# The first weight fetches and the first chunk's k on ScalarE's DMA queue, six raw weight tiles instead of three

## The chip, the cores and the metric

The kernel runs on one core of a Trainium2 chip, as one launch. The metric is the device time of an execution in microseconds; the time before is the median of three runs, and one more execution was taken with the hardware profiler. The core has five engines that run in parallel and each work through their own instructions in order: TensorE (PE, with the weight load PEld shown apart), VectorE (DVE), ScalarE (ACT), GpSimd (POOL) and SyncE (SP). They wait for one another through semaphores. Transfers between HBM and SBUF are done by 16 DMA engines; an instruction on the queue of an engine, up to now always SP, issues them.

## The reference

Three stages follow each other, all in float32 (the weights come as float64):

```python
# 1: retention, 8 batches, 8 heads, 576 positions, head dimension 64
scores = np.matmul(q, k.transpose(0, 1, 3, 2)) / np.sqrt(64)
ret = scores * Dmat            # gamma[h] ** (i - j) for i >= j, else 0
x = np.matmul(ret, v)          # -> (4608, 512)
# 2: maxout layer, w1, w2, w3 (512, 768), w_out (768, 512)
h = np.maximum(np.maximum(x @ w1, x @ w2), x @ w3)
x = h @ w_out
# 3: bilinear layer, w1, w2 (512, 1024), w3 (1024, 1024), w_out (1024, 512)
out = ((x @ w1) * (x @ w2) @ w3) @ w_out
```

## The kernel before

**Work.** The 4608 tokens are taken in nine blocks of 512. The retention is computed in chunks of 128 or 64 positions with a carried state. The chunks are counted from 0 here: 0 to 3 have 128 positions each and fill the first block; chunk 4, the rest of the first batch, has 64. For each block the maxout layer then runs over six feature blocks f of 128 features and three weights i. Every product is done in three passes of split numbers: x is split into a high part xh and a rest xl, a weight into w1h and w1l (`products`, L332 to L341).

**A chunk.** `attend` records for each chunk: the fetch of q and k, four pieces each (`fetch_qk`, L233), of v and of kn, which is k with positions on the partitions (`fetch_kv`, L243); the scaling of q on POOL (L249); the transposes of q and k on VectorE into qt and kt (L256); the scores on PE (L262); the decay on VectorE (L266); the state product st on PE (L281) and, on VectorE, its addition to the carried state (L287) and the scaling of the state (L289); two copies of the state into `wide` on ScalarE (L293); the output o on PE (L271, L275); and the split of o into xh on ScalarE (L75 from L296) and xl on VectorE (L78 from L300).

**A weight unit.** The weights are float64 and are turned to float32 by `convert` (L120). A unit is 512 columns of 128 rows: `fetch` loads the raw 64-bit words into a tile named raw, in two DMAs of half the partitions; `words` makes two float tiles e and l from them on ScalarE (L134, L135); `scale` and `join` work on VectorE and, for some units, on POOL (L140 to L148); `done` splits the result w into w1h on ScalarE (L75) and w1l on VectorE or POOL (L78). There are 18 units of the first layer, unit 3f + i for feature block f and weight i. The tag raw has three buffers, so a fetch waits until the unit three places ahead of it in fetch order has been joined.

**What sets the order.** Each step is put on a list with a time number by `when` (L113); the list is sorted by it, and the steps are emitted in that order, so every engine's queue has a fixed order. The numbers of the startup stand in tables (`CHUNK_AT`, `W1_AT`, `W1_FETCH`, `HALF_AT`); the fetch of a unit has its own time, often far ahead of its work. All transfers go through `load` (L80) on SP.

**Completion counters.** Each DMA raises one of eight counters (DMAHW0 to DMAHW7) when it has landed. They are handed out in turn to the DMAs as they are emitted, whichever queue issues them, and a DMA waits on its queue until the preceding DMA with the same counter has landed. So a DMA can wait for another one with which it shares nothing else, and everything behind it on its queue waits too.

Of the kernel before, what the change touches and what calls it, by code (L numbers as in the profile page):

```python
# [11 lines left out]
I32 = mybir.dt.int32  # L12
# [10 lines left out]
P = 128  # L23
# [6 lines left out]
HALF_AT = [-6.14, -4.03, -0.84, -1.51, -0.17, 1.3, -0.43, 1.91, 3.01, -0.35, 2.74, 6.39]  # L30
L_DVE = [0, 0, 0, 0, 1, 0, 1, 1, 1, 0, 0, 0, 1, 0, 1, 1, 1, 1]
LO_DVE = [0, 0, 0, 0, 0, 0, 1, 0, 0, 0, 0, 0, 1, 1, 0, 0, 1, 1]
BACC = dict(dynamic_dma_scratch_size=512)


# [34 lines left out]
def tile_retention_maxout_bilinear(ctx: ExitStack, tc, a, out):  # L70
    nc = tc.nc
# [5 lines left out]
    def low(eng, dst, full, hi):  # L77
        eng.tensor_tensor(dst, full, hi.bitcast(F32), ALU.subtract)  # L78

    def load(dst, src):  # L80
        nc.sync.dma_start(out=dst, in_=src)  # L81

    first_ps = ctx.enter_context(ExitStack())
    ps_mm = first_ps.enter_context(tc.tile_pool(name="ps_mm", bufs=4, space=PSUM))
# [32 lines left out]
    T_BLK = 3 * KF1  # L117


    def convert(t, loads, done, eng=nc.gpsimd, lead=3):  # L120

        z = {}

        def fetch():
            z["raw"] = cv.tile([P, 1024], I32, tag="raw", name="raw", bufs=3)
            for dst, src in loads(z["raw"]):
                load(dst, src)

        def words():
            raw = z["raw"].rearrange("p (n t) -> p n t", t=2)  # L130
            z["hi"] = raw[:, :, 1]
            z["e"] = cv.tile([P, 512], F32, tag="e", name="e")
            z["l"] = cv.tile([P, 512], F32, tag="l", name="l")
            nc.scalar.activation(z["e"], raw[:, :, 1].bitcast(F32), AF.Copy, scale=2.0 ** -112)  # L134
            nc.scalar.activation(z["l"], raw[:, :, 0].bitcast(U32), AF.Copy, scale=2.0 ** -52)  # L135

        def scale():
            z["m"] = cv.tile([P, 512], I32, tag="m", name="m")
            e = z["e"].bitcast(I32)
            nc.vector.tensor_scalar(z["m"], e, 3, None, ALU.logical_shift_left)  # L140
            nc.vector.tensor_scalar(e, e, 3, 0x7F800000, ALU.logical_shift_left, ALU.bitwise_and)  # L141
            eng.tensor_tensor(z["l"], z["l"], z["e"], ALU.mult)  # L142

        def join():
            m = z["m"].bitcast(F32)
            nc.vector.tensor_tensor(m, m, z["l"], ALU.add)  # L146
            w = cv.tile([P, 512], I32, tag="w", name="w")
            nc.vector.scalar_tensor_tensor(w, z["hi"], -0x80000000, z["m"], ALU.bitwise_and, ALU.bitwise_or)  # L148
            z["w"] = w.bitcast(F32)

        when(t - lead, fetch)
        when(t - 1, words)
        when(t, scale)
        when(t + 1, join)
        when(t + 2, lambda: done(t + 2, z["w"]))
# [10 lines left out]
    def w1_unit(t, f, i, eng, eng2, lead):  # L166
        src = words_of(f"moe_w{i + 1}")[:, 2 * f * P:2 * (f + 1) * P].rearrange("(g c p) e -> g p c e", g=2, p=D)

        def loads(raw):
            r = raw.rearrange("p (c e) -> p c e", c=4)  # L170
            return [(r[D * g:D * g + D], src[g]) for g in range(2)]

        def done(t, w):
            copy_r(flat(w1h[f][:, i]), w)
            low(eng, flat(w1l[f][:, i]), w, flat(w1h[f][:, i]))

        convert(t, loads, done, eng2, lead)

    def rows_unit(t, src, dst):
        convert(t, lambda raw: [(raw, src)], lambda t, w: load(dst, w))  # L180
# [45 lines left out]
    def attend(n, t, t_st):  # L226
# [4 lines left out]
        z = {}  # L231

        def fetch_qk():  # L233
            z["q"] = at.tile([P, 4, G, 32], F32, tag="q", name="q", bufs=3)
            z["k"] = at.tile([P, 4, G, 32], F32, tag="k", name="k", bufs=3)
            for x in "qk":
                for g in range(2):
                    for e in range(2):
                        o = D * g + 32 * e
                        load(z[x][o:o + 32, :r], a[x][b, G * g:G * g + G, t0:t0 + c, 32 * e:32 * e + 32].rearrange(  # L240
                            "h (t T) d -> t T h d", T=r))

        def fetch_kv():  # L243
            for x in ("v",) if last else ("v", "kn"):
# [670 lines left out]
```

## Time and profile before

| | us |
|---|---|
| median of three runs (1381.56 to 1383.19) | 1382.69 |
| the profiled execution | 1383.29 |
| its span, first to last instruction | 1381.5 |
| PE busy | 1324.6 (96%) |
| VectorE busy | 821.9 (59%) |
| ScalarE busy | 469.5 (34%) |
| POOL busy | 498.4 (36%) |

The shares are means over very different stretches: the page's row of PE over 40 equal slices of 34.5 us begins with 3, 6, 8, 8 tenths and has 9 in nearly all others, while the row of VectorE begins with 3, then 9, 9, 9. A row of a view in order of time has the start in us from the beginning of the span, the duration, the engine, the line, the operation, the tile written and the tiles read, the shapes, how many instructions are merged in it, and in brackets the idle time of the engine ahead of it with what ended it. SPq rows are the issues of DMAs on SP's queue; they say nothing of when the data has landed.

### The profile page before, as it was taken

The page shows a single profiled execution, that of the slowest core. Times are in us where ns is not written, and L with a number is a line of the kernel's source. Part 1 is how long each engine was busy: PE and PEld are TensorE (multiplying, and loading weights), DVE is VectorE, ACT ScalarE, POOL GpSimd, SP SyncE. Part 2 cuts the span into 40 slices and gives each one's busy share as a digit, 9 for nine tenths or more (in the row PEclk, how much of TensorE's full clock was granted, in tenths as well). Part 3 has the DMA queues.
Part 4 walks back from the last instruction along what each step waited for, and adds up shares of the span by engine and source line. Part 5 has one row for each costly group of instructions (what it writes and reads, how often), then busy time and mean ns, then how long its engine had stood idle before and what let it go on. Part 6 is the DMA issues. An engine that isn't in the chain of part 4 may idle for free.

```text
span 1381.5 us, 23689 instructions
## 1 busy us (share of the span) xinstructions
PE 1324.6 (96%) x8904; PEld 1207.1 (87%) x8904; DVE 821.9 (59%) x1205; ACT 469.5 (34%) x933; POOL 498.4 (36%) x419
## 2 busy tenths in 40 slices
PE   3688999999999999999999999999999999899998
PEld 3676887888887888889999989999999999899998
DVE  3999677676676777423662343343343336688885
ACT  1433222322322222112543343332333324355553
POOL 2552233233223232113753343343343334444442
PEclk9799999999999999999999999999999999999999
DMA  8878678767777779234656542222223222445452
GB/s 149 156 156 167 161 172 185 179 162 181 170 179 165 151 152 197 66 107 147 207 177 218 175 159 94 81 75 81 75 75 104 75 91 74 127 148 167 153 168 93
DMA packets 368580, 194.09 MB, mean 140 GB/s; under 512 B 263888, under 2 KB 342352, under 8 KB 368464
## 3 DMA queue, kind: packets, MB, share of 16 engines
q1 hardware_dynamic: 368464, 192.57, 52.8%
q8 instruction: 70, 1.15, 0.4%
q14 instruction: 46, 0.38, 0.1%
HBM read 126.44 MB, written 66.06 MB: 139 GB/s over the span
## 4 chain that ended last, share of the span: by engine, by line
PE 86%; DVE 3%; DMA 2%; issue 1%; ACT 1%; SPq 0%; POOL 0%; DVEq 0%; ACTq 0%
PE ps_h L340 30%; PE ps_x L499 21%; PE ps_y L499 11%; PE ps_z L499 9%; PE ps_v L499 5%; PE ps_w L499 3%; PE sc L262 2%; PE o L271 2%; PE o L275 2%; PE st L281 1%; DMA raw<-in_moe_w_dram 1%; DMA z_d<-zo 0%; DMA gr<-g_d 0%; DMA hr<-h_d 0%; SPq L81 0%
## 5 line engine op out<-in xcount | busy, mean ns | idle before, releaser
L340 PE MATMUL ps_h<-xh,w1h 128*128 128x512 f32 (+1 forms) x672 | 264.5, 396 | 5.2 <-ACT xh L75 3.3
L340 PE MATMUL ps_h<-xh,w1l 128*128 128x512 f32 (+1 forms) x672 | 257.7, 385 | 3.1 <-POOL w1l L78 1.8
L142 POOL TENSOR_TENSOR l<-l,e 128x512 f32<-128x512 f32 x55 | 70.8, 1288 | 332.6 <-DVE e L141 276.3
L340 PE MATMUL ps_h<-xl,w1h 128*128 128x512 f32 (+1 forms) x672 | 175.5, 383 | 0.0
L340 PEld LDWEIGHTS ps_h<-xh,w1h 128*128 128x128 f32 x672 | 127.4, 190 | 37.6 <-issue 4.4
L340 PEld LDWEIGHTS ps_h<-xh,w1l 128*128 128x128 f32 x672 | 127.6, 190 | 27.2 <-POOL w1l L78 2.3
L340 PEld LDWEIGHTS ps_h<-xl,w1h 128*128 128x128 f32 x672 | 124.6, 189 | 24.9 <-DVE xl L78 0.2
L351 DVE TENSOR_TENSOR hb<-ps_h,hb 128x512 f32<-128x512 f32 (+1 forms) x112 | 74.6, 668 | 117.3 <-PE ps_h L340 103.9
L794 POOL TENSOR_TENSOR c<-c 128x384 f32<-128x384 f32 x72 | 81.5, 1132 | 171.1 <-DVE c L663 87.7
L658 ACT ACTIVATE snap<-ps_x 128x384 f32<-128x384 f32 x120 | 58.7, 491 | 197.4 <-PE ps_x L499 195.2
L499 PE MATMUL ps_z<-hh,w1oh 128*128 128x384 f32 x288 | 96.3, 334 | 0.8 <-issue 0.8
L499 PE MATMUL ps_z<-hl,w1oh 128*128 128x384 f32 x288 | 96.3, 334 | 0.2 <-DVE hl L78 0.2
L499 PE MATMUL ps_z<-hh,w1ol 128*128 128x384 f32 x288 | 96.2, 334 | 0.0
L75 ACT ACTIVATE hb<-ps_h 128x512 f32<-128x512 f32 (+1 forms) x56 | 32.4, 580 | 177.5 <-PE ps_h L340 177.4
L146 DVE TENSOR_TENSOR m<-m,l 128x512 f32<-128x512 f32 x64 | 70.1, 1095 | 16.5 <-POOL l L142 16.5
L134 ACT ACTIVATE e<-raw 128x512 f32<-128x512 f32 x64 | 42.9, 670 | 100.4 <-DMA raw<-in_moe_w_dram 82.1
L78 POOL TENSOR_TENSOR hl<-hr,hh 128x384 fp32r<-128x384 f32 x36 | 39.4, 1093 | 79.0 <-ACT hh L75 77.8
L262 PEld LDWEIGHTS sc<-qt,kt 64*128 64x128 f32 (+1 forms) x640 | 38.1, 187 | 32.5 <-issue 20.7
L262 PE MATMUL sc<-qt,kt 64*128 64x128 f32 (+1 forms) x640 | 45.7, 284 | 21.6 <-DVE kt L256 20.3
L663 DVE TENSOR_TENSOR c<-ps_v,snap 128x384 f32<-128x384 f32 x48 | 26.7, 557 | 62.1 <-PE ps_v L499 40.1
L256 DVE STREAM_TRANSPOSE qt<-q 128x512 f32<-128x512 f32 (+1 forms) x40 | 38.5, 961 | 31.3 <-POOL q L249 18.6
L148 DVE SCALAR_TENSOR_TENSOR w<-raw,m 128x512 int32<-128x512 int32 x64 | 55.2, 862 | 2.7
(214 smaller groups left out, 3536.1 us busy)
## 6 DMA issues: line engine op xcount, KB each, us to landing
g_d<-c SPq DMA_DIRECT2D x96, 192.0 KB, 1.9
h_d<-hb SPq DMA_DIRECT2D x54, 256.0 KB, 3.0
gr<-g_d SPq DMA_DIRECT2D x12, 1024.0 KB, 5.8
raw<-in_moe_w_dram SPq DMA_DIRECT2D x36, 256.0 KB, 4.4
z_d<-zo SPq DMA_DIRECT2D x12, 768.0 KB, 3.6
zr<-z_d SPq DMA_DIRECT2D x48, 192.0 KB, 3.1
out_dram<-ob SPq DMA_DIRECT2D x36, 256.0 KB, 2.1
q<-in_q_dram SPq DMA_DIRECT2D x128, 64.0 KB, 3.9
```

What stands on the lines that cost most here:

```text
L78: eng.tensor_tensor(dst, full, hi.bitcast(F32), ALU.subtract)
L134: nc.scalar.activation(z["e"], raw[:, :, 1].bitcast(F32), AF.Copy, scale=2.0 ** -112)
L142: eng.tensor_tensor(z["l"], z["l"], z["e"], ALU.mult)
L146: nc.vector.tensor_tensor(m, m, z["l"], ALU.add)
L148: nc.vector.scalar_tensor_tensor(w, z["hi"], -0x80000000, z["m"], ALU.bitwise_and, ALU.bitwise_or)
L256: nc.vector.transpose(out=z[x + "t"][:, :, :c].rearrange("p h (t T) -> p T h t", T=r), in_=z[x][:, :r])
L262: nc.tensor.matmul(z["sc"][g][:c, h, :c], z["kt"][rows, h, :c], z["qt"][rows, h, :c], start=True, stop=True)
L340: nc.tensor.matmul(ps[:, cols], l, r, start=n == 0, stop=n == len(mms) - 1)
L351: nc.vector.tensor_tensor(hb, ps[:, cols], hb, ALU.max)
L499: nc.tensor.matmul(ps, l, r, start=start and j == 0, stop=stop and j == len(mms) - 1, skip_group_check=again)
L658: nc.scalar.activation(t, ps[:, :N2], AF.Copy)
L794: nc.gpsimd.tensor_tensor(x, x, y, ALU.mult)
```

## The change

`load` gets a queue as a parameter, SP by default. The raw fetches of the weight units 0 to 7 and the four k pieces of chunk 0 are issued on ScalarE's queue, at the same places of the sorted list as before. The tag raw has six buffers instead of three. No arithmetic changes, and the order of the instructions on PE, VectorE and POOL is the same.

```diff
+N_ACT = 8
...
-    def load(dst, src):
-        nc.sync.dma_start(out=dst, in_=src)
+    def load(dst, src, queue=nc.sync):
+        queue.dma_start(out=dst, in_=src)
...
-    def convert(t, loads, done, eng=nc.gpsimd, lead=3):
+    def convert(t, loads, done, eng=nc.gpsimd, lead=3, queue=nc.sync):
...
-            z["raw"] = cv.tile([P, 1024], I32, tag="raw", name="raw", bufs=3)
+            z["raw"] = cv.tile([P, 1024], I32, tag="raw", name="raw", bufs=6)
             for dst, src in loads(z["raw"]):
-                load(dst, src)
+                load(dst, src, queue)
...
-        convert(t, loads, done, eng2, lead)
+        convert(t, loads, done, eng2, lead, nc.scalar if 3 * f + i < N_ACT else nc.sync)
...
                         load(z[x][o:o + 32, :r], a[x][b, G * g:G * g + G, t0:t0 + c, 32 * e:32 * e + 32].rearrange(
-                            "h (t T) d -> t T h d", T=r))
+                            "h (t T) d -> t T h d", T=r), nc.scalar if n == 0 and x == "k" else nc.sync)
```

**ScalarE at the start.** In the rows that follow a name has the number of its buffer; raw_169, raw_185 and raw_205 are the raw tiles of the first three units fetched, wide0 and xh_201<-o_188 belong to chunk 0. Before:

```order
L293 ACT_TABLE_LOAD [waits DVE_49]
L293 ACTIVATE wide0_132<-s_197 64x256 [waits Pool_49]
L293 ACTIVATE wide0_132<-s_197 64x256
L75 ACTIVATE xh_201<-o_188 128x4x128 [waits PE_49]
L134 ACTIVATE e_261<-raw_205 128x512 [waits DMAHW7_49,DMAHW0_49]
L135 ACTIVATE l_262<-raw_205 128x512
L134 ACTIVATE e_284<-raw_169 128x512 [waits DMAHW4_49,DMAHW3_49]
L135 ACTIVATE l_285<-raw_169 128x512
```

After:

```order
L82 DMA k_140<-in_k_dram 32x16x32 x4
L82 DMA raw_169<-in_moe_w2_dram 64x4x256 [waits DMAHW1_49]
L82 DMA raw_169<-in_moe_w2_dram 64x4x256 [waits DMAHW3_49]
L82 DMA raw_185<-in_moe_w3_dram 64x4x256 [waits DMAHW5_49]
L82 DMA raw_185<-in_moe_w3_dram 64x4x256 [waits DMAHW7_49]
L295 ACT_TABLE_LOAD [waits DVE_49]
L295 ACTIVATE wide0_132<-s_197 64x256 [waits Pool_49]
L295 ACTIVATE wide0_132<-s_197 64x256
L76 ACTIVATE xh_201<-o_188 128x4x128 [waits PE_49]
L82 DMA raw_205<-in_moe_w1_dram 64x4x256 [waits DMAHW5_49]
L82 DMA raw_205<-in_moe_w1_dram 64x4x256 [waits DMAHW7_49]
L135 ACTIVATE e_261<-raw_205 128x512 [waits DMAHW7_49,DMAHW5_49]
```

Eight DMA issues stand ahead of ScalarE's first instruction, and the two halves of raw_205 between the xh copy of chunk 0 and the first work on a weight. The two halves of raw_205 use the counters DMAHW5 and DMAHW7.

**SP at chunk 2.** q_227 and k_228 are the q and k of chunk 2. Before:

```order
L81 DMA q_227<-in_q_dram 32x16x32 [waits DMAHW3_49]
L81 DMA q_227<-in_q_dram 32x16x32 [waits DMAHW4_49]
L81 DMA q_227<-in_q_dram 32x16x32 [waits DMAHW5_49]
L81 DMA q_227<-in_q_dram 32x16x32 [waits DMAHW6_49]
L81 DMA k_228<-in_k_dram 32x16x32 [waits DMAHW7_49]
L81 DMA k_228<-in_k_dram 32x16x32 [waits DMAHW0_49]
L81 DMA k_228<-in_k_dram 32x16x32 [waits DMAHW1_49]
L81 DMA k_228<-in_k_dram 32x16x32 [waits DMAHW2_49]
```

After:

```order
L82 DMA q_227<-in_q_dram 32x16x32 [waits DMAHW3_49]
L82 DMA q_227<-in_q_dram 32x16x32 [waits DMAHW4_49]
L82 DMA q_227<-in_q_dram 32x16x32 [waits DMAHW5_49]
L82 DMA q_227<-in_q_dram 32x16x32 [waits DMAHW6_49]
L82 DMA k_228<-in_k_dram 32x16x32 [waits DMAHW7_49]
L82 DMA k_228<-in_k_dram 32x16x32 [waits DMAHW0_49]
L82 DMA k_228<-in_k_dram 32x16x32 [waits DMAHW1_49]
L82 DMA k_228<-in_k_dram 32x16x32 [waits DMAHW2_49]
```

The pieces and the names of their counters are the same; which DMA had each counter last is not. Before, all eight waited for pieces of chunk 1 on SP's own queue. Now DMAHW5 and DMAHW7 were last given to the two halves of raw_205 on ScalarE's queue, and the third q piece and the first k piece wait for those.

**ScalarE and SP at chunk 4.** v_322 and kn_324 belong to chunk 3, q_345 and k_346 to chunk 4, the one with 64 positions; wide0_132<-s_410 are the copies of the state after chunk 2. SP before:

```order
L81 DMA v_322<-in_v_dram 128x8x64 [waits DMAHW5_49,PE_49,Pool_49]
L81 DMA kn_324<-in_k_dram 128x8x64 [waits DMAHW6_49]
L81 DMA raw_342<-in_moe_w1_dram 64x4x256 [waits DMAHW7_49,DVE_49,Activation_49]
L81 DMA raw_342<-in_moe_w1_dram 64x4x256 [waits DMAHW0_49]
L81 DMA q_345<-in_q_dram 32x8x32 [waits DMAHW1_49,Pool_49]
L81 DMA q_345<-in_q_dram 32x8x32 [waits DMAHW2_49]
L81 DMA q_345<-in_q_dram 32x8x32 [waits DMAHW3_49]
L81 DMA q_345<-in_q_dram 32x8x32 [waits DMAHW4_49]
L81 DMA k_346<-in_k_dram 32x8x32 [waits DMAHW5_49]
L81 DMA k_346<-in_k_dram 32x8x32 [waits DMAHW6_49]
L81 DMA k_346<-in_k_dram 32x8x32 [waits DMAHW7_49]
L81 DMA k_346<-in_k_dram 32x8x32 [waits DMAHW0_49]
```

SP after:

```order
L82 DMA v_322<-in_v_dram 128x8x64 [waits DMAHW7_49,PE_49,Pool_49]
L82 DMA kn_324<-in_k_dram 128x8x64 [waits DMAHW0_49]
L82 DMA q_345<-in_q_dram 32x8x32 [waits DMAHW1_49,DVE_49]
L82 DMA q_345<-in_q_dram 32x8x32 [waits DMAHW2_49]
L82 DMA q_345<-in_q_dram 32x8x32 [waits DMAHW4_49]
L82 DMA q_345<-in_q_dram 32x8x32 [waits DMAHW5_49]
L82 DMA k_346<-in_k_dram 32x8x32 [waits DMAHW7_49,DVE_49]
L82 DMA k_346<-in_k_dram 32x8x32 [waits DMAHW0_49]
L82 DMA k_346<-in_k_dram 32x8x32 [waits DMAHW1_49]
L82 DMA k_346<-in_k_dram 32x8x32 [waits DMAHW3_49]
```

ScalarE after:

```order
L295 ACTIVATE wide0_132<-s_410 64x256 [waits DVE_49,Activation_49]
L295 ACTIVATE wide0_132<-s_410 64x256 [waits Activation_49]
L82 DMA raw_442<-in_moe_w2_dram 64x4x256 [waits DMAHW3_49]
L82 DMA raw_442<-in_moe_w2_dram 64x4x256 [waits DMAHW6_49]
L76 ACTIVATE xh_201<-o_387 128x4x128 [waits PE_49]
L82 DMA raw_454<-in_moe_w3_dram 64x4x256 [waits DMAHW2_49]
L82 DMA raw_454<-in_moe_w3_dram 64x4x256 [waits DMAHW5_49]
```

Before, the fourth k piece (DMAHW0) waited for the second half of raw_342, the raw fetch that stood ahead of it on SP. Now it waits on DMAHW3, which the first half of raw_442 raises; that fetch stands on ScalarE behind the `wide` copies of the state after chunk 2, s_410. The v of chunk 3 (v_322, DMAHW7) and the first q piece of chunk 4 (DMAHW1) now wait for the two halves of raw_342 on ScalarE.

## Rows read from the trace of the kernel before

**Rows 1.** three stretches: length, busy PE PEld DVE ACT POOL, PEclk, DMA share, GB/s

```profile
0.00:31.90 31.90, 10.88 (x112) 9.51 (x112) 10.16 (x13) 5.01 (x8) 6.41 (x11) 1.00 0.82 152
31.90:136.70 104.80, 84.33 (x709) 70.59 (x709) 101.49 (x147) 41.62 (x77) 49.99 (x38) 0.87 0.80 157
136.70:1381.50 1244.80, 1229.44 (x8085) 1127.04 (x8083) 710.30 (x1047) 422.87 (x848) 442.03 (x370) 1.00 0.50 139
```

**Rows 2.** VectorE in order of time: start, duration, instruction

```profile
133.20 0.68 DVE L78 TENSOR_TENSOR w1l<-w,w1h 128x512 fp32r<-128x512 f32 x1
```

**Rows 3.** PE in order of time; in brackets idle before and releaser

```profile
62.50 0.45 PE L340 MATMUL ps_h<-xh,w1h 128*128 128x256 f32 x1 [3.33 <-ACT xh L75]
...
117.90 0.50 PE L340 MATMUL ps_h<-xh,w1l 128*128 128x512 f32 x1 [1.25 <-DVE w1l L78]
...
122.34 0.50 PE L340 MATMUL ps_h<-xh,w1h 128*128 128x512 f32 x1 [1.66 <-ACT w1h L75]
123.70 0.50 PE L340 MATMUL ps_h<-xh,w1l 128*128 128x512 f32 x1 [0.85 <-POOL w1l L78]
...
133.94 0.50 PE L340 MATMUL ps_h<-xh,w1l 128*128 128x512 f32 x1
```

**Rows 4.** VectorE in order of time, 0 to 50 us

```profile
8.49 1.08 DVE L256 STREAM_TRANSPOSE kt<-k 128x512 f32<-128x512 f32 x1 [0.21 <-DMA k<-in_k_dram]
...
13.77 0.42 DVE L289 TENSOR_TENSOR s<-st,tables 128x256 f32<-128x256 f32 x1 [0.75 <-PE st L281]
...
30.81 1.08 DVE L256 STREAM_TRANSPOSE kt<-k 128x512 f32<-128x512 f32 x1 [1.20 <-DMA k<-in_k_dram]
...
41.73 1.12 DVE L256 STREAM_TRANSPOSE qt<-q 128x512 f32<-128x512 f32 x1 [0.39 <-POOL q L249]
...
44.85 1.36 DVE L289 TENSOR_TENSOR s<-sum,tables 128x256 f32<-128x256 f32 x1
...
48.98 0.40 DVE L256 STREAM_TRANSPOSE kt<-k 128x256 f32<-128x256 f32 x1
```

**Rows 5.** SP's DMA issues in order of time

```profile
1.18 2.76 SPq L81 DMA_DIRECT2D q<-in_q_dram  x4
...
25.15 2.68 SPq L81 DMA_DIRECT2D k<-in_k_dram  x4
```

**Rows 6.** POOL in order of time

```profile
6.11 1.05 POOL L249 TENSOR_TENSOR q<-q,tables 128x512 f32<-128x512 f32 x1 [4.40 <-DMA q<-in_q_dram]
...
38.95 1.73 POOL L78 TENSOR_TENSOR w1l<-w,w1h 128x512 fp32r<-128x512 f32 x1 [2.02 <-ACT w1h L75]
```

**Rows 7.** ScalarE in order of time

```profile
16.45 0.60 ACT L75 ACTIVATE xh<-o 128x512 fp32r<-128x512 f32 x1
...
46.31 0.86 ACT L293 ACTIVATE wide<-s 64x256 f32<-64x256 f32 x2 [1.78 <-DVE s L289]
...
120.07 0.66 ACT L134 ACTIVATE e<-raw 128x512 f32<-128x512 f32 x1 [4.09 <-DMA raw<-in_moe_w_dram]
```

**Rows 8.** DMA issues, 0 to 60 us: count, KB each, median us to landing

```profile
raw<-in_moe_w_dram SPq DMA_DIRECT2D x15, 256.0 KB, 4.4
...
k<-in_k_dram SPq DMA_DIRECT2D x20, 64.0 KB, 2.7
...
kn<-in_k_dram SPq DMA_DIRECT2D x5, 256.0 KB, 5.1
...
k<-in_k_dram SPq DMA_DIRECT2D x4, 32.0 KB, 2.3
...
tables<-in_tables_dram SPq DMA_DIRECT2D x1, 88.0 KB, 1.9
```

**Rows 9.** DMA issues, 40 to 46 us

```profile
raw<-in_moe_w_dram SPq DMA_DIRECT2D x1, 256.0 KB, 4.1
```

**Rows 10.** the same columns, two stretches with the clock

```profile
124.40:128.00 3.60, 3.60 (x11) 2.57 (x9) 3.50 (x7) 2.25 (x4) 1.13 (x1) 0.56 0.47 67
62.50:66.00 3.50, 3.50 (x15) 3.30 (x16) 3.43 (x8) 1.37 (x3) 1.36 (x2) 0.53 1.25 209
```


## The prediction

> **What bounds the kernel now.** I read the utilisation of three stretches first, then PE's and VectorE's time-ordered instructions at the end of the startup, then the four other engines and the DMA queue backwards from there. The utilisation shows where a change of the first fetches can count at all [rows 1]: from 136.7 us to the end PE is busy 1229.44 of 1244.80 us, so the rest of the program costs the same whenever it begins. In the first 31.9 us VectorE works only 10.16 us, waiting for data. Between 31.9 and 136.7 us VectorE is busy 101.49 of 104.80 us, an in-order stream with 3.3 us of gaps over some 147 instructions. That stream sets the end of the startup: its last but one w1l piece ends at 133.88 us [rows 2], and PE, waiting in order, takes it at 133.94 us [rows 3] (the stretch of rows 1 is cut where the last such piece ends). PE's earlier idle times, 1.25, 1.66 and 0.85 us at 117.90, 122.34 and 123.70 us [rows 3], only let it fall back onto a stream that it meets again at 133.9 us. So the question is by how much VectorE's stream is shifted after its last wait for data. In this trace that is the transpose of chunk 2's k at 30.81 us, which waited 1.20 us for its DMA [rows 4]; after it one wait of 0.39 us stands, at 41.73 us.
>
> **Chunk 0: k leaves SP's queue.** SP issues the four q pieces from 1.18 to 3.94 us, 0.69 us each, and q is scaled on POOL at 6.11 us [rows 5, 6]. The k transpose at 8.49 us comes behind the q transpose on VectorE, so an earlier k is worth at most its wait of 0.21 us [rows 4]. The fourth q piece now waits on the completion counter of the first k piece, which is issued with SP's first transfer and lands a median 2.7 us later [rows 8], some 0.3 us after the q piece would have gone. I take 0 for the transposes. v and kn move up by about 2 us of SP time, so PE's state product follows the scores directly: VectorE's scaling of the state at 13.77 us, which waited 0.75 us for it [rows 4], starts 0.7 us earlier, and the chain behind it on ScalarE (table load, two copies, x_hi at 16.45 us for 0.60 us [rows 7]) ends at 16.3 instead of 17.05 us. The four early raw fetches on ScalarE stand where ScalarE is idle and cost nothing.
>
> **Chunk 2: the stream starts earlier.** SP has sixteen raw issues and four k issues less, so chunk 1 arrives early enough not to bind. Chunk 2 is tied to ScalarE by a shared completion counter: its third q piece waits until the first half of the raw tile fetched behind x_hi has landed. That fetch is issued at 16.3 us; raw fetches land a median 4.4 us after issue [rows 8], so 20.7 us. Six issues follow, two of q and four of k, 0.65 us apart; the last is issued at 20.7 + 5 x 0.65 = 24.0 us, and k lands a median 2.7 us later [rows 8], at 26.7 us. In this trace the same piece took 3.6 us (the four issues span 25.15 to 27.83 us [rows 5], the transpose starts at 30.81). I take 27.0 us against 30.81: a gain of 3.8 us.
>
> **ScalarE's own delay.** Two raw issues now stand between the second x_hi and the first w1h copy, 1.3 us of ScalarE time of which 0.65 us is covered by waiting for VectorE. POOL's w1l piece waits for that copy (38.95 us, idle 2.02 us) [rows 6], POOL's next q scaling stands behind it, and VectorE's transpose at 41.73 us waits for that scaling [rows 4]. So 0.65 us of the 3.8 is given back: 3.15 us remain.
>
> **Chunk 4: the new wait.** The last piece of the short chunk's k waits on a counter that now belongs to the raw fetch behind the `wide` copies of ScalarE. Before, it waited for the preceding raw fetch of SP's own queue, and the transpose at 48.98 us never waited [rows 4]. Now: the scaling of the state (44.85 us, 1.36 us long [rows 4]) ends at 46.21 - 3.15 = 43.06; the `wide` copies, 0.10 us behind it and 0.86 us long [rows 7], end at 44.0; the raw half lands 4.2 us later (between the median of 4.4 of the first 60 us and the 4.1 of a raw fetch at this place [rows 8, 9]), at 48.2; the k piece of 32 KB lands 2.3 us after issue [rows 8], at 50.5; the transpose starts at 50.6 us. That is 1.65 us later than 48.98. Behind it on VectorE stands the entire rest of the stream, and POOL, ScalarE and PE wait for that. The gain of 3.15 us is turned into a loss of 1.65 us, since a path of 2.8 us between state scaling and transpose (46.21 to 48.98) becomes one of 7.5 us.
>
> **Six raw tiles.** SP's later raw fetches no longer wait for a tile, and ScalarE's wait of 4.09 us for one at 120.07 us [rows 7] goes. It hid w1h and w1l copies on which PE idled 1.66 + 0.85 us, but the stream at 133.9 us is late next, and it has no wait for a raw tile in it. I take 0. The later fetches on the two queues (chunks 5 and 6) land, by the same steps, some microseconds before VectorE comes to them, even with their waits for the remaining raw fetches on ScalarE.
>
> **Sum.** 0 (chunk 0) - 3.8 + 0.65 + (7.5 - 2.8 = 4.7) + 0 = +1.6 to +1.7 us. The profiled execution lasted 1383.29 us around a span of 1381.5, 0.60 us above the median of 1382.69. Its span would become 1383.2, the execution 1385.0, the median 1384.4 us.
>
> **Bounds.** No DMA is issued by ScalarE in this trace, so its landing time is open. From below, 1.9 us (the 88 KB table, the shortest of [rows 8]) instead of 4.4 and 4.2, and issue beside the running copy instead of after it (0.6 and 0.86 us): 1.65 - 2.5 - 2.3 - 1.4 = -4.6 us. From above, 5.1 us (kn) for both raw fetches and 3.6 us for both k: +0.7 + 0.6 + 0.9 + 1.3, which gives +5.1 us. I stay at the medians of the raw rows, which are the same transfer. The Trainium skill, page "DMA: Bandwidth & Descriptors", section "Issuing engines are not separate DMA queues", says that transfers of both queues run on the same 16 engines and that a second issuer saves issue time alone; by that the landing times would stay the raw rows' own, as in the sum.
>
> **Rivals.** (1) Faster. A raw fetch on a queue of its own does not stand behind q and k pieces and lands in about 2 us, and is issued while the copy runs. Place: both hops behind ScalarE; it decides when raw fetches land under 3 us. Each hop gains about 2.2 us: 1.65 - 4.4 - 0.6 = -3.3 us, 1379.4 us. For it: the DMA share was high early (0.82 [rows 1]), so queues were long. Against: at 40 to 46 us, with less traffic, a raw fetch still took 4.1 us [rows 9]. (2) Slower: two queues issue no faster than one. If 0.65 us is a shared generator's time, the eight q and k pieces of chunk 0 take turns, the last q is issued by 1.18 + 8 x 0.65 = 6.4 instead of 3.94 us, and chunk 0's chain, on which both hops hang, runs some 2.2 us late: +3.9 us, 1386.6 us. For it: issue times vary little with bytes. Against: a time that hardly depends on the transfer may as well be the issuer's own. The Trainium skill, page "Perfetto Trace Analysis", section "DMA Instruction — HWDGE (DVE, Sync)", says that a DMA locks a shared descriptor generator before it uses it; no row here shows two issuers. (3) Slower: the clock. With the wait at 120 us gone PE no longer idles at 122.34 us, reaches the w1l piece of 133.94 us about 3 us before it, and idles there. After an idle of 3.33 us at 62.50 us [rows 3] the granted clock was 0.53 for 3.5 us, close to the lower level of 1.2 GHz; after the 1.66 and 0.85 us it was 0.56 for 3.6 us [rows 10]. Now nothing behind PE's last idle hides that: half of 3.6 us less what overlaps, about 1.6 us more: +3.2 us, 1385.9 us. Against: the idle may be spread over several pieces, as it is now.
>
> **Numbers.** A change of 0.2% is 2.8 us, about what can be told from none here. Forecast 0.42 (own range 1382.7 to 1386), of it 0.33 within 0.2% and 0.09 slower; rival 1 0.18 (0.14 faster, 0.04 within); rival 2 0.19 (0.14 slower, 0.05 within); rival 3 0.21 (0.15 slower, 0.06 within). Faster 0.14, same 0.48, slower 0.38. The range runs from rival 1's 1379.4, rounded in to 1379.8, to 1387.8, the upper bound of the landing times (1382.7 + 5.1).
>
> **What will show it.** The k transpose of chunk 2 at about 27 us and that of chunk 4 at 50 to 51 us, with an idle of some 4.5 us before it put down to a k DMA; SP's queue standing still from some 14 to 20.7 us and again until 48 us; the wait of 4.09 us at 120 us gone; PE's last idle at w1l of the last feature block instead of the fifth. If chunk 4's transpose starts before 46.2 us the forecast is wrong toward faster; if raw fetches on ScalarE land after 5 us, or chunk 0's k transpose starts after 10 us, toward slower.

## The result and the profile after

The changed kernel takes 1389.95 us (median of 4 runs, 1388.69 to 1391.42) against 1382.94 us (4 runs, 1381.56 to 1383.35): ratio 1.0055, interval 1.0043 to 1.0068, so 7.0 us slower. The forecast had the direction, slower, but its 1384.4 us and its range up to 1387.8 were too low. The profiled execution lasted 1388.69 us, the shortest of the four, with a span of 1386.9 us, 5.4 above that of before.

VectorE in order of time, with start, duration and in brackets the idle time and its releaser; the last row is the w1l piece of [rows 2]:

```profile
9.16 1.05 DVE L258 STREAM_TRANSPOSE kt<-k 128x512 f32<-128x512 f32 x1
...
14.37 0.42 DVE L291 TENSOR_TENSOR s<-st,tables 128x256 f32<-128x256 f32 x1 [0.70 <-PE st L283]
...
28.92 1.08 DVE L258 STREAM_TRANSPOSE kt<-k 128x512 f32<-128x512 f32 x1 [0.67 <-DMA k<-in_k_dram]
...
39.83 1.13 DVE L258 STREAM_TRANSPOSE qt<-q 128x512 f32<-128x512 f32 x1 [0.38 <-POOL q L251]
...
42.96 1.36 DVE L291 TENSOR_TENSOR s<-sum,tables 128x256 f32<-128x256 f32 x1
...
55.27 0.45 DVE L258 STREAM_TRANSPOSE kt<-k 128x256 f32<-128x256 f32 x1 [8.11 <-DMA k<-in_k_dram]
...
139.40 0.68 DVE L79 TENSOR_TENSOR w1l<-w,w1h 128x512 fp32r<-128x512 f32 x1
```

Read against [rows 4]: chunk 0's k transpose is 0.67 us later, chunk 2's 1.89 earlier (28.92 for 30.81), and that gain is still whole at 39.83 (41.73) and 42.96 (44.85). Then chunk 4's k transpose, 48.98 before without a wait, starts at 55.27 after 8.11 us of idle time. From there the stream keeps its lateness: 6.29 us at 55.27, 6.20 at 139.40 (133.20 in [rows 2]). The whole loss stands in front of one 0.45 us transpose.

ScalarE in order of time; ACT rows are its engine's instructions, ACTq rows the fetches issued from its queue:

```profile
16.08 0.65 ACTq L82 DMA_DIRECT2D raw<-in_moe_w_dram  x1
16.17 0.85 ACT L295 ACTIVATE wide<-s 64x256 f32<-64x256 f32 x2
16.77 0.64 ACTq L82 DMA_DIRECT2D raw<-in_moe_w_dram  x1
...
44.42 0.42 ACT L295 ACTIVATE wide<-s 64x256 f32<-64x256 f32 x1 [3.85 <-DVE s L291]
44.47 0.60 ACTq L82 DMA_DIRECT2D raw<-in_moe_w_dram  x1
...
45.12 0.63 ACTq L82 DMA_DIRECT2D raw<-in_moe_w_dram  x1
45.79 0.60 ACT L76 ACTIVATE xh<-o 128x512 fp32r<-128x512 f32 x1 [0.52 <-issue]
45.81 1.27 ACTq L82 DMA_DIRECT2D raw<-in_moe_w_dram  x2
47.13 0.38 ACT L76 ACTIVATE hb<-ps_h 128x256 f32<-128x256 f32 x1 [0.74 <-issue]
47.21 1.27 ACTq L82 DMA_DIRECT2D raw<-in_moe_w_dram  x2
48.53 0.63 ACT L76 ACTIVATE w1h<-w 128x512 fp32r<-128x512 f32 x1 [1.01 <-issue]
```

Six halves of 256 KB, those of units 4, 5 and 6, are issued in one burst from 44.47 to 48.48 us. A fetch goes out beside the copy ahead of it, but each copy behind a fetch starts only when its issue has ended, after 0.52, 0.74 and 1.01 us of idle time. SP's queue at the same time:

```profile
20.73 1.92 SPq L82 DMA_DIRECT2D q<-in_q_dram  x1
...
41.91 6.71 SPq L82 DMA_DIRECT2D k<-in_k_dram  x4
...
48.03 0.58 SPq L82 DMA_DIRECT2D k<-in_k_dram  x1
```

(the 48.03 row is the last of the four at 41.91). The DMA issues of short stretches, with count, KB each and median us from issue to landing: the fourth k piece of chunk 4 falls into the last stretch, 48 to 49 us, and k's third one into the first, 43.2 to 44.1. The second stretch, 44.1 to 44.8, holds unit 4's first half. The rows of ScalarE's queue (q10: packets, MB, share of the 16 engines) are of 44 to 56 us and of 48.03 to 55.1 us.

```profile
k<-in_k_dram SPq DMA_DIRECT2D x1, 32.0 KB, 2.4
...
raw<-in_moe_w_dram ACTq DMA_DIRECT2D x1, 256.0 KB, 3.5
...
q10 hardware_dynamic: 1632, 1.57, 58.1%
...
q10 hardware_dynamic: 1091, 1.04, 70.5%
...
raw<-in_moe_w_dram ACTq DMA_DIRECT2D x1, 256.0 KB, 6.9
v<-in_v_dram SPq DMA_DIRECT2D x1, 128.0 KB, 6.9
k<-in_k_dram SPq DMA_DIRECT2D x1, 32.0 KB, 7.0
```

The last k piece waits for unit 4's first half (44.47 + 3.5 = 47.97), is issued at 48.03 and lands at 55.0: 7.0 us for 32 KB that took 2.4 us when issued five microseconds before. While it is under way, ScalarE's queue moves 1.04 of the burst's 1.57 MB. With it land all that was issued at that time, from either queue: a raw half 6.9, v 6.9. Busy times of the engines in three stretches, columns as in [rows 1], show the hole and the full DMA engines:

```profile
44.00:48.00 4.00, 4.00 (x48) 3.61 (x47) 3.12 (x4) 1.81 (x4) 2.25 (x3) 1.00 0.60 149
48.00:52.00 4.00, 0.34 (x12) 0.20 (x8) 0.00 (x0) 1.84 (x3) 0.00 (x0) 0.80 1.07 224
52.00:56.00 4.00, 0.00 (x0) 0.00 (x0) 0.73 (x2) 0.00 (x0) 0.00 (x0) 0.50 1.01 129
```

At the end of the startup PE still waits for VectorE's stream, at other places than before ([rows 3]), and goes on at the upper clock level, 2.4 GHz, after its last idle time (1.00 in the second window row, columns as above); the first is behind its idle time of 2.04 us:

```profile
131.64 1.19 PE L273 MATMUL o<-p,v 64*64 64x64 f32 x16 [2.04 <-DVE p L268]
...
140.14 0.50 PE L342 MATMUL ps_h<-xh,w1l 128*128 128x512 f32 x1 [1.10 <-DVE w1l L79]
```

```profile
133.60:135.20 1.60, 1.60 (x18) 1.48 (x16) 1.57 (x2) 0.00 (x0) 1.60 (x2) 0.50 0.05 18
...
140.10:144.00 3.90, 3.86 (x17) 3.10 (x18) 3.67 (x8) 0.89 (x2) 0.00 (x0) 1.00 0.20 69
```

### The profile page after: what moved, and what is told of

Read it like the earlier page. It is cut to its first block, busy times and chain, and to the rows that moved or that the text cites. A ratio compares the mean times of both kernels' runs of the same rounds, so it can differ in the third digit from the quotient of the medians.

```text
span 1386.9 us, 23687 instructions
## 1 busy us (share of the span) xinstructions
PE 1325.8 (96%) x8904; PEld 1209.4 (87%) x8904; DVE 822.7 (59%) x1205; ACT 469.7 (34%) x933; POOL 499.6 (36%) x419
## 4 chain that ended last, share of the span: by engine, by line
PE 87%; DVE 1%; DMA 0%; issue 0%; ACT 0%; POOL 0%; DVEq 0%; ACTq 0%
PE ps_h L342 30%; PE ps_x L501 21%; PE ps_z L501 11%; PE ps_y L501 11%; PE ps_v L501 5%; PE ps_w L501 3%; PE sc L264 2%; PE o L273 2%; PE o L277 1%; PE st L283 1%; DMA gr<-g_d 0%; DVE w L695 0%; DVE gr L732 0%; POOL a22l L79 0%; DVE a12l L79 0%
## 5 line engine op out<-in xcount | busy, mean ns | idle before, releaser
L665 DVE TENSOR_TENSOR c<-ps_x,snap 128x384 f32<-128x384 f32 x48 | 25.5, 552 | 52.0 <-PE ps_x L501 47.5
```

Source lines behind the costliest of these rows:

```text
L665: nc.vector.tensor_tensor(r, ps[:, :N2], t, ALU.add)
```

## The experiments

Ratios are to runs of the kernel before made beside each kernel (medians 1382.31 to 1382.94), with 95% intervals, and are worked out from all runs, so they can differ from the ratio of two medians. k times are the starts of VectorE's transposes in the profiled execution, w1l that of the piece of [rows 2]. 0.001 is 1.4 us. The profiled executions are within 1.3 us of their kernel's median, but for no_wait (1388.32, 3.2 above) and no_wait_light (1387.37, 1.8 above).

| kernel | median us | ratio | k of chunk 0 | chunk 2 | chunk 4 (wait) | w1l |
|---|---|---|---|---|---|---|
| before | 1382.94 | 1 | 8.49 | 30.81 | 48.98 (0) | 133.20 |
| changed | 1389.95 | 1.0055 (1.0043 to 1.0068) | 9.16 | 28.92 | 55.27 (8.11) | 139.40 |
| raws_only | 1391.55 | 1.0065 (1.0051 to 1.0079) | 12.30 | 29.45 | 55.88 (8.19) | 141.12 |
| scalar_three_tiles | 1391.21 | 1.0062 (1.0050 to 1.0075) | 9.53 | 29.32 | 54.28 (6.34) | 141.15 |
| light_burst | 1386.74 | 1.0031 (1.0020 to 1.0043) | 9.10 | 29.29 | 52.02 (4.49) | 136.99 |
| no_wait | 1385.10 | 1.0027 (1.0016 to 1.0038) | 10.89 | 30.00 | 51.09 (2.86) | 136.82 |
| no_wait_light | 1385.61 | 1.0020 (1.0011 to 1.0028) | 11.21 | 30.49 | 49.67 (0.95) | 135.91 |
| later_56 | 1384.82 | 1.0020 (1.0010 to 1.0029) | 10.40 | 28.58 | 46.76 (0) | 133.60 |
| five_units | 1384.09 | 1.0017 (1.0008 to 1.0026) | 9.75 | 28.74 | 46.92 (0) | 133.27 |
| six_tiles | 1383.64 | 1.0006 (0.9998 to 1.0015) | 8.66 | 31.28 | 49.44 (0) | 134.48 |
| four_units | 1382.86 | 1.0003 (0.9995 to 1.0012) | 9.38 | 28.96 | 47.12 (0) | 132.20 |
| three_units | 1382.12 | 1.0002 (0.9994 to 1.0011) | 10.81 | 29.49 | 47.66 (0) | 132.55 |
| two_units | 1381.23 | 0.9994 (0.9985 to 1.0002) | 10.38 | 28.21 | 46.36 (0) | 131.49 |
| three_early | 1381.74 | 0.9993 (0.9985 to 1.0002) | 9.51 | 27.32 | 45.45 (0) | 130.33 |
| kv_on_scalar | 1380.23 | 0.9987 (0.9979 to 0.9996) | 9.66 | 27.27 | 45.42 (0) | 129.82 |
| k_alone | 1380.55 | 0.9985 (0.9976 to 0.9994) | 9.30 | 28.09 | 46.24 (0) | 131.31 |
| k_alone_three_tiles | 1379.86 | 0.9981 (0.9972 to 0.9990) | 9.11 | 27.67 | 45.83 (0) | 130.53 |

**Six tiles alone** (six_tiles). The kernel before, with

```diff
-            z["raw"] = cv.tile([P, 1024], I32, tag="raw", name="raw", bufs=3)
+            z["raw"] = cv.tile([P, 1024], I32, tag="raw", name="raw", bufs=6)
```

> The kernel before with six raw tiles and every fetch still on SP's queue. My theory: the loss comes from ScalarE's fetches alone, so nothing here: 1382.9 us within 1.5, transposes of chunk 2's and chunk 4's k at 30.8 and 49.0 us as before. Rival, the tiles themselves do it: with six tiles SP no longer holds raw fetches back, they stand in front of chunk 4's and 5's q and k in time, chunk 4's k transpose waits at 49 us or later, and the time is 1386 us or more.

Ratio 1.0006, and no wait at chunk 4: the tiles by themselves do not make the loss. The profile starts chunk 2 0.47 us late; that the tiles cost this much can't be told.

**A light burst** (light_burst). Units 5 and 6 fetch one of four column blocks, which is read four times; three quarters of their weights are left out.

```diff
-            return [(r[D * g:D * g + D], src[g]) for g in range(2)]
+            n = 1 if 3 * f + i in (5, 6) else 4
+            return [(r[D * g:D * g + D, :n], src[g, :, :n]) for g in range(2)]
...
```

> The changed kernel, with the same fetches on the same queues in the same order; only the fetches of weight units 5 and 6, which ScalarE issues right behind unit 4's, carry a quarter of their bytes (three quarters of these two units' weights are left out and the quarter is read four times). Chunk 4's last k piece still waits for unit 4's first half. Theory 1, wait and burst together: the piece is issued at about 48 us as in the changed kernel but lands within 2.3 to 3 us instead of 7.0, the k transpose of chunk 4 starts at 50.5 to 51.5 us instead of 55.3, and the time falls by 4 to 5 us to about 1385.5. Theory 2, the wait alone, with the burst beside it harmless: transpose at 55 us, 1390 us.

Of its trace VectorE's row, SP's last k piece and that piece's landing:

```profile
52.02 0.45 DVE L264 STREAM_TRANSPOSE kt<-k 128x256 f32<-128x256 f32 x1 [4.49 <-DMA k<-in_k_dram]
```

```profile
49.57 0.58 SPq L82 DMA_DIRECT2D k<-in_k_dram  x1
```

```profile
k<-in_k_dram SPq DMA_DIRECT2D x1, 32.0 KB, 2.3
```

The piece still waits for unit 4 (issued 44.85, landed 4.7 later), but it lands in 2.3 us instead of 7.0. Theory 1 holds in its mechanism; the transpose is 0.5 us later than its bracket and the time 1.2 us above it (3.2 us back, not 4 to 5). So the 7.0 us are the burst that was under way. Two limits: bytes and packets fell together, so which of them counts is not shown; and unit 6's fetch, in the changed kernel issued ahead of the piece (47.21 us), goes out at 50.29 us here, behind it.

**No wait** (no_wait). For chunk 4 alone, k's first piece as two DMAs:

```diff
-                        load(z[x][o:o + 32, :r], a[x][b, ...].rearrange("h (t T) d -> t T h d", T=r), ...)
+                        src = a[x][b, ...].rearrange("h (t T) d -> t T h d", T=r)
+                        for T in ([slice(0, 1), slice(1, 2)] if n == 4 and x == "k" and g == e == 0 else [slice(0, r)]):
+                            load(z[x][o:o + 32, T], src[:, T], ...)
```

> The changed kernel, with the first k piece of chunk 4 fetched in two DMAs instead of one (halves by time step). That adds one issue on SP (0.65 us) and one place in the row of completion counters: the last k piece of chunk 4 then waits for a q piece of its own chunk instead of ScalarE's fetch of unit 4. ScalarE's burst of six 256 KB fetches from 44.5 us on stays. Theory 1, wait and burst together: the pieces are all issued by 45.2 us, ahead of most of the burst, land by 48.5 us, the transpose of chunk 4's k starts at 47.5 to 48.8 us, the 1.9 us won at chunk 2 is mostly kept, and the time is 1381 to 1384. Rival, the burst alone holds up whatever is in flight: transpose at 51 us or later, 1385 us or more.

One more DMA in the row of completion counters gives back 4.9 us by the medians, 3.9 by the ratios. Theory 1 missed place and time; the rival's bounds are met, both at their edge (51.09 for 51 us, 1385.10 for 1385). But the place is that of an execution of 1388.32 us, and the burst did not stay. VectorE, the DMAs issued about the last k piece (46 to 46.6 us), and ScalarE, whose fetch of unit 5 now waits for unit 4's landing (it shares the counter) and holds up the copies behind it:

```profile
51.09 0.45 DVE L259 STREAM_TRANSPOSE kt<-k 128x256 f32<-128x256 f32 x1 [2.86 <-DMA k<-in_k_dram]
```

```profile
raw<-in_moe_w_dram ACTq DMA_DIRECT2D x2, 256.0 KB, 4.7
v<-in_v_dram SPq DMA_DIRECT2D x1, 128.0 KB, 6.5
k<-in_k_dram SPq DMA_DIRECT2D x1, 32.0 KB, 5.2
```

```profile
49.24 3.25 ACTq L82 DMA_DIRECT2D raw<-in_moe_w_dram  x2
52.53 0.38 ACT L76 ACTIVATE hb<-ps_h 128x256 f32<-128x256 f32 x1 [5.06 <-DMA raw<-in_moe_w_dram]
```

The last k piece is issued at 45.71 us, between unit 4's two halves (45.55 and 46.20), and takes 5.2 us. The edit replaced one wait by another and put units 5 and 6 behind the piece, so it changed wait and burst together: what the wait costs by itself it does not show.

**Only the weights on ScalarE** (raws_only): `nc.scalar if n == 0 and x == "k" else nc.sync` becomes `nc.sync`.

> The changed kernel with chunk 0's k back on SP's queue; the eight weight units stay on ScalarE's, six tiles, and the wait of chunk 4's last k piece for unit 4 is there. My theory: k's part is worth nothing at the end: chunk 4's k transpose at 54 to 56 us and 1389 to 1391 us. In the changed kernel q of chunk 0 landed 1.0 us later (POOL's scaling at 7.15 instead of 6.11 us); if that came from k issued beside it, it is 6.1 us again here, if from the raw fetches, it stays near 7.1. Rival, the later chunk 0 is what the rest hangs on: 1388 us or less, with chunk 4's transpose earlier by that 1 us.

1391.55 us and chunk 4 at 55.88, as my theory had it to within 0.6 us. Chunk 0's q did neither of the two: it was scaled at 10.29 us. Its third piece, issued at 2.63 us as in the changed kernel and with no wait, lands at 9.7 us, beside the first four weight halves; the fourth waits for the first of these and goes out at 4.63 instead of 3.55 us. The third piece (issues of 2.9 to 3.2 us):

```profile
q<-in_q_dram SPq DMA_DIRECT2D x1, 64.0 KB, 7.1
```

So a small piece lands late beside large ones here too. Of the 3.1 us more at chunk 0 only 0.5 come through to chunk 2, which hangs on the third unit's fetch.

**Fewer units on ScalarE** (four_units, three_units; `N_ACT = 4` and `N_ACT = 3`).

> The changed kernel with four weight units on ScalarE's queue instead of eight: units 4 to 7 go back to SP's, so nothing large is issued beside chunk 4's k and its last piece waits for nothing of ScalarE's. Theory 1, the whole loss is made at chunk 4 (wait, then a landing behind 1.5 MB): chunk 4's k transpose starts without a wait at 47 to 48 us, the 1 to 1.9 us won at chunk 2 stay, and the time is 1380.5 to 1382.5, faster than before. Theory 2, the early fetches beside chunk 0 cost as well (its q lands 1 to 2.7 us late in the runs so far) and the gain at chunk 2 is gone in most runs: 1382.5 to 1384, chunk 2's k transpose near 30 us.

> The changed kernel with three weight units on ScalarE's queue, those fetched before chunk 3; from unit 3 on SP fetches. Against four units it takes away the tie of chunk 4's q and chunk 3's v to a fetch behind ScalarE's work. Theory 1: chunk 4's transpose at 47 to 48 us and 1380.5 to 1382.5, equal to four units within 1 us, since the tie at chunk 3 shows no wait on VectorE above 0.4 us. Theory 2 as for four units: 1382.5 to 1384.

The wait at chunk 4 is gone and with it 7.1 us (1389.95 to 1382.86): units 4 to 7 on ScalarE's queue are the whole loss. Chunk 4's place is theory 1's in both; the time of four_units lies in theory 2's bracket, that of three_units in theory 1's. No gain on before can be told for either (1.0003 and 1.0002), though in both profiles chunk 2 is 1.3 to 1.9 us early and w1l 0.7 to 1.0.

**k alone** (k_alone; `N_ACT = 0`, six tiles), and the same with three tiles (k_alone_three_tiles).

> The kernel before with six raw tiles and chunk 0's k alone on ScalarE's queue; all weight units on SP's. SP has four issues (2.67 us) less ahead of chunk 1 and 2. If SP's issue time is what chunk 2's k waits for: its transpose at 28.2 to 29 us instead of 30.8 and 1380.5 to 1382. If it is the traffic on the DMA engines: at 30 to 31 us and 1382.5 to 1384. Chunk 0's k transpose, behind the scaled q of 6.1 us: q near 6.1 if the raw fetches made it late in the changed kernel, near 7.1 if k's did.

> The kernel before with chunk 0's k alone on ScalarE's queue and three raw tiles: one line of the change. With six tiles it took 1380.55 us. Theory: the tiles are worth nothing either way (six tiles alone: ratio 1.0006, 0.9998 to 1.0015), so 1379.5 to 1381.5, faster than before by 0.1 to 0.2%. Rival, the gain needs both: 1382 to 1383.

Both are faster than before; with three tiles 1379.86 us. That SP's issue time is what chunk 2's k waited for fits: its transpose is 2.7 to 3.1 us earlier for four issues (2.67 us) less. Of k_alone_three_tiles:

```profile
27.67 1.08 DVE L258 STREAM_TRANSPOSE kt<-k 128x512 f32<-128x512 f32 x1 [0.90 <-DMA k<-in_k_dram]
...
45.83 0.40 DVE L258 STREAM_TRANSPOSE kt<-k 128x256 f32<-128x256 f32 x1
```

```profile
7.09 1.05 POOL L251 TENSOR_TENSOR q<-q,tables 128x512 f32<-128x512 f32 x1 [5.37 <-DMA q<-in_q_dram]
```

q of chunk 0 is 1.0 us late ([rows 6]) with no weight fetch on ScalarE's queue, so k issued beside it does that much.

**Units 5 and 6 later** (later_56).

```diff
-... -6.38, -5.9, -5.79, -2.95, ...
+... -6.38, -4.0, -3.9, -2.95, ...
```

> The changed kernel with the fetches of units 5 and 6 due at -4.0 and -3.9 instead of -5.9 and -5.79: they stand 2 to 10 instructions later on ScalarE, still on its queue, and chunk 4's last k piece no longer shares a counter with unit 4's fetch. Unit 4's two halves (0.5 MB) are still issued beside chunk 4's last k pieces. Theory: as in the run without the wait, k lands behind these two halves in 4 to 5 us instead of 2.3, its transpose waits 2 to 3 us and starts at 49 to 51 us; 1383 to 1385.5. Rival, without the wait nothing is lost: at 47 to 48 us, 1381 to 1382.5.

My place was wrong: chunk 4's k, all issued by 44.14 us, before ScalarE's first fetch, is not late. The time was in its bracket, but what the profile shows is further on: chunk 5's k, now beside units 5 and 6, lands late (issue of 51.6 us) and its transpose waits.

```profile
46.76 0.40 DVE L258 STREAM_TRANSPOSE kt<-k 128x256 f32<-128x256 f32 x1
...
61.65 1.08 DVE L258 STREAM_TRANSPOSE kt<-k 128x512 f32<-128x512 f32 x1 [1.99 <-DMA k<-in_k_dram]
```

```profile
k<-in_k_dram SPq DMA_DIRECT2D x1, 64.0 KB, 6.6
```

That takes back 1.9 of the 2.2 us won at chunk 4 (61.65 for 62.02 us before), and w1l is 0.4 us late. The median's 2.3 us over before are more than this, and the rest is not accounted for.

**Wait and burst together** (no_wait_light): the edits of no_wait and light_burst in one kernel.

> Both edits of the runs without the wait and with the light burst together, in the changed kernel: chunk 4's last k piece doesn't wait for unit 4, and units 5 and 6 fetch a quarter of their bytes (three quarters of these two units' weights are left out). Unit 4's 0.5 MB still goes out on ScalarE's queue beside chunk 4's k. If wait and burst are two parts of one delay: against the changed kernel the wait alone gave back 4.9 us and the light burst alone 3.2; both together can't give more than the 7.1 us of four units, so 1383 to 1384.5, with chunk 4's k transpose at 47 to 50 us. If they are separate and add up (8.1 us): 1382 or less. If the light burst adds nothing once the wait is gone: 1385.

1385.61 us: once the wait is gone the lighter burst adds nothing that can be told, as the last of the three expectations had it; in no_wait units 5 and 6 were already behind the piece. Its chunk 4 waits 0.95 us instead of 2.86; the rest of its lateness was there before (chunk 2 at 30.49), and ScalarE stands still for unit 5's counter as in no_wait (4.82 us).

**All on ScalarE, three tiles** (scalar_three_tiles): the changed kernel with `bufs=3`.

> The changed kernel with three raw tiles as before; all its fetches on ScalarE's queue. The fetches of units 5 and 6 then wait for a tile (for VectorE's joins of earlier units) and can't go out in one burst with unit 4's, but ScalarE itself stands still in that wait, with its copies behind it. Chunk 4's last k piece waits for unit 4's first half as in the changed kernel. Theory 1, the six tiles let the burst happen: chunk 4's k lands 2.3 to 4 us after its issue, transpose at 50.5 to 52.5 us, 1385 to 1388. Rival, ScalarE's standing still costs more than the burst: 1389 us or more.

The rival was right. Unit 6's fetch is held back, but ScalarE stands still for 11 us with its copies behind it, and chunk 4's last k piece, issued at 49.61 us with three of four halves still under way, lands 4.5 us after issue:

```profile
58.69 1.27 ACTq L82 DMA_DIRECT2D raw<-in_moe_w_dram  x2
60.00 0.63 ACT L76 ACTIVATE w1h<-w 128x512 fp32r<-128x512 f32 x1 [11.00 <-issue]
```

```profile
k<-in_k_dram SPq DMA_DIRECT2D x1, 32.0 KB, 4.5
```

**The third unit early** (three_early; `N_ACT = 3`, its `W1_FETCH` -22.8 for -20.7) and **two units** (two_units; units 1 and 2 on ScalarE, `3 * f + i in (1, 2)`).

> Three weight units on ScalarE's queue and the third of them fetched ahead of ScalarE's first work (due at -22.8 instead of -20.7), so that chunk 2's q and k no longer wait for a fetch that stands behind ScalarE's x_hi. Three units took 1382.1, k alone 1380.55. Theory 1, the 1.6 us between them is that tie: chunk 2's k transpose at 26.5 to 28 us instead of 29.5, 1379 to 1380.5. Theory 2, it is the traffic of the early fetches beside chunk 0's q (8.8 us instead of 6.1): chunk 0 no earlier than 8.5 us, chunk 2 at 28 to 29.5, 1380.5 to 1382.5.

> Chunk 0's k and the two weight units fetched first on ScalarE's queue, the third one (whose fetch stands behind ScalarE's x_hi in the changed kernel) back on SP's queue. k alone 1380.55, three units 1382.1, three early 1381.7. Theory 1, early traffic beside chunk 0's q is what three units lose against k alone: 1381 to 1382.5, chunk 0's q scaled at 7 to 9 us. Theory 2, it is the tie of chunk 2 to the third unit's fetch: 1379.5 to 1381, chunk 2's k transpose near 28 us.

Without the tie chunk 2's k starts at 27.32 and 28.21 instead of 29.49: the tie delays chunk 2, as one theory had it, and the times (1381.74 and 1381.23) lie in the other's brackets. Both medians stay 0.7 to 1.2 us above k_alone's, and the intervals overlap with k_alone's and with three_units'. What the tie costs in time, and how tie and traffic share it, stays open.

**Five units** (five_units; `N_ACT = 5`).

> The changed kernel with five weight units on ScalarE's queue; units 5 to 7 on SP's. Unit 4 (0.5 MB) is issued by ScalarE beside chunk 4's last k pieces as in the changed kernel, but chunk 4's k waits for no counter of ScalarE's, and no fetch of ScalarE's stands behind unit 4's. With the wait gone 1385.1 us were left, with the burst light as well 1385.6; four units take 1382.9. Theory 1, the 2.3 us left are unit 4's fetch beside k: chunk 4's k transpose 1 to 3 us behind its q's end, 1384 to 1385.5. Theory 2, they are the fetch of unit 5, which in those runs waits on ScalarE for unit 4's landing and holds up ScalarE's copies for 5 us: gone here, transpose without a wait, 1382 to 1383.5.

Neither theory: the transpose has no wait (against theory 1), the time is 0.6 us above theory 2's bracket (it lies in theory 1's). After chunk 4 VectorE has one wait of 0.4 us up to w1l, but the same instructions are busy longer. The stretch from chunk 4's k transpose to the w1l piece, first of before, then of five_units, third busy number VectorE:

```profile
48.98:133.20 84.22, 69.44 (x596) 58.00 (x596) 81.76 (x120) 33.97 (x63) 38.78 (x29) 0.92 0.85 166
```

```profile
46.92:133.27 86.35, 70.26 (x593) 59.23 (x593) 83.62 (x120) 34.32 (x63) 40.47 (x29) 0.90 0.87 167
```

120 instructions take 1.86 us more, which is most of the 2.1 us won at chunk 4. Why they run longer was not tried.

**v and kn too** (kv_on_scalar): k_alone_three_tiles with `nc.scalar if n == 0 else nc.sync` for the fetches of v and kn.

> The fastest kernel so far (chunk 0's k alone on ScalarE's queue, three raw tiles, 1379.9 us) with chunk 0's v and kn there as well: SP has two issues (1.25 us) less ahead of chunk 1. If SP's issue still sets chunk 2's arrival: its k transpose 0.5 to 1.2 us earlier than 27.7, 1378.5 to 1380. If the DMA engines are the bound by now: unchanged, 1379.5 to 1381.

Chunk 2 0.4 us earlier, the time the same within the intervals: SP's issue is no longer the only bound there.

## Why the prediction was wrong, step by step

**Bound.** Right: VectorE's stream after its last wait sets the end; 6.29 us at chunk 4 are 6.20 at w1l and 5.4 of the span.

**Chunk 0: 0.** Small miss, +0.67 us: q lands 1.0 us later beside k. x_hi did not have to end for the third unit's fetch: it was issued at 16.08, beside `wide` and ahead of x_hi's run, so the forecast 16.3 was right by luck, by another way.

**Chunk 2: gain 3.8.** Half of it came. The third q piece is issued at 20.73 us (forecast 20.7), but by luck: the half that it waits for landed at 20.46, and SP had not stood still, since chunk 2's first q piece took 2.35 us to issue and the second ended at 20.69. The third then took 1.92 us instead of 0.65. The sum also left a wait out: the first k piece waits for the second half of the same fetch, as the list in "The change" shows, and the forecast had it issued at 22.0. That half, issued at 16.77 us, landed at 23.15 (issues of 17.0 to 17.3 us); in three_units, where SP was free, it landed at 24.34 and the piece went out at 24.36. In the changed kernel:

```profile
raw<-in_moe_w_dram ACTq DMA_DIRECT2D x1, 256.0 KB, 6.4
```

The first k piece went out at 23.38, the last at 25.42 (forecast 24.0), and landed in 3.3 us instead of 3.0: 28.92 instead of 27.0.

**ScalarE's own delay: 0.65 given back.** Wrong, 0: the 1.89 us of chunk 2 arrive whole at 39.83 us. There the two fetches (34.33 to 35.60 us) go out beside running copies, and the w1h copy behind them waits for VectorE until 36.36 as it did before. In the burst the copies do wait for the issues, while VectorE waits for k.

**Chunk 4.** Forecast and trace: raw half issued 44.0 and 44.47, landed 48.2 and 47.97; k issued 48.2 and 48.03; k landed 50.5 and 55.0. The wait came within 0.3 us of the forecast, by luck: the scaling of the state ended 1.3 us later than forecast (44.32 for 43.06), and the fetch, issued beside the copies and landing in 3.5 us, took 1.5 us less. The step that failed is "the k piece of 32 KB lands 2.3 us after issue": 7.0. That median was of pieces with little under way; here 1.04 MB of ScalarE's burst still had to move. The path from the end of the state scaling to the transpose became 10.95 us instead of 7.5 (2.77 before). Sum: -1.89 + 0 + 8.18 = +6.29 for +1.65. light_burst shows the cause of the long landing (2.3 again, 3.2 us back), four_units that wait and burst together are the whole loss (7.1). no_wait took 4.9 us back by changing both.

**Six tiles: 0.** Alone, yes. But they are what lets ScalarE issue six halves in 4 us without a wait for a tile; I counted only the waits they take away (the one of 4.09 us at 120 us is gone), not what they let loose. That three tiles were no cure is scalar_three_tiles' 11 us.

**Upper bound.** It took 3.6 us for k, which is from one piece's issue to its transpose (3.4 to its landing). The trace before has longer ones, which the medians of [rows 8] hide: the last k piece of chunk 3 (34.52 us) took 4.5 us, and chunk 1's first q piece, issued at 12.83 us behind six raw halves on SP's own queue, 6.6:

```profile
q<-in_q_dram SPq DMA_DIRECT2D x1, 64.0 KB, 6.6
```

With 6.6 us for chunk 4's piece the upper bound is 3.0 us higher, 1390.8, above the 1389.95 measured (an estimate from these rows). The price stood in the trace, in the rows of pieces behind a burst.

**Rivals.** (1) Raw fetches in 2 us: no, 3.5 us at 44.47 and 6.9 at 47.85, at the end of the burst. (2) One shared generator: ScalarE's four k pieces (0.74 to 3.54 us) and SP's four q pieces (1.18 to 4.13) went out side by side, 0.70 and 0.74 us each, where the rival had eight in turn, 5.2 us. Chunk 0 was late by 0.67, not 2.2 (the rival's own steps, 6.4 less 3.94, give 2.4). The section "DMA Instruction — HWDGE (DVE, Sync)" of the Trainium skill's "Perfetto Trace Analysis" says that a DMA locks the shared generator for exclusive use. Here the eight issues took 3.4 us together, at most 0.42 us of it for each (an estimate), so a lock over the whole of an issue is excluded; a shorter one is not. (3) The clock: PE's last idle time is indeed at a w1l piece, 1.10 us at 140.14, but the clock after it is 1.00. The longer idle time, 2.04 us at 131.64, did bring the lower level (0.50 from 133.60 to 135.20 us), ahead of that last wait and not behind it. The section "Issuing engines are not separate DMA queues" of the Trainium skill's "DMA: Bandwidth & Descriptors" says that DMAs of all issuers run on the same 16 engines and interleave. The trace agrees: the small piece on SP's queue landed with the last half on ScalarE's (7.0 us from 48.03, 6.9 from 47.85). What the prediction drew from it, landing times that stay the raw rows' own, did not hold.

**Against the kernel before,** then: chunk 0's k on ScalarE is worth -2.0 us with six tiles (0.9985; three tiles 0.9981), the first four units beside it cost 2.3, so all of that, and units 4 to 7 cost 7.1.

## What to carry to other kernels

Price a transfer's landing by what is in flight at its issue, from all queues, and not by the median of its kind. Chunk 4's last k piece landed in 2.3, 4.5, 5.2 and 7.0 us while ScalarE's queue moved 0.12, 0.53, 0.54 and 1.04 MB (light_burst, scalar_three_tiles, no_wait, changed); a longer landing also leaves more time to move bytes, so this is an order and not a price per byte. When a fetch is moved to an engine's queue, ask what the same event releases with it: here the copies ahead of unit 4's fetch and the next two copies let 1.5 MB out within 4 us, and the piece that waited for the first half was issued behind the other five. What a second queue is good for is issue time on a chain that waits for issues: moving four small DMAs (k alone, six tiles) gained 2.0 us, moving the eight weight fetches as well cost 9.4.

## What was not expected of the hardware

A DMA issued from ScalarE's queue does not wait for the copies that stand ahead of it to run: 16.08 us against `wide` from 16.17 and x_hi behind that. A copy behind it does wait until the issue has ended (0.52 to 1.01 us idle in the burst). An issue on SP can itself take 1.92 us instead of 0.65 (20.73 us, DMA share 1.27); full engines alone do not do it, since from 49.71 us, at a share of 1.14, issues took 0.6 us each. What does stays open. And chunk 0's q was scaled at times from 7.1 to 9.2 us in kernels whose instructions up to there are the same (light_burst 7.09, no_wait_light 9.20); with one profile of each, what decides it stays open.
